# The first 128 tokens of expert 0 are gathered from three batches, and their two layers are issued inside the gating of the last batch

## Chip, cores, metric

The kernel runs on one core of a Trainium2 chip. The metric is the device time of one execution in microseconds; the kernel before has 881.16 us as the median of three runs (878.74 to 881.35). Its trace comes from one further execution under the profiler.

## What is computed

Three parts follow each other. Attention with a decay bias over 4 batches, 8 heads, 576 positions and 64 per head; its output is a matrix x of 2304 tokens by 512. Then a mixture of 8 experts in which every token goes to one expert, and its result is scaled by a gate:

```python
logits = x @ w_gate
e_idx = np.argmax(logits, axis=1)
...
for e in range(E):
    mask = e_idx == e
    h = np.maximum(x[mask] @ w1[e], 0.0)
    ye = h @ w2[e]
    out[mask] = gate_w[mask, None] * eom[mask, e, None] * ye
```

Here w1[e] is 512 x 1024 and w2[e] is 1024 x 512. Last, a feed-forward part over all tokens: h = x @ w_in (512 x 2048), g = relu(h) squared, out = g @ w_out. The weights w_in and w_out arrive as 64-bit floats.

## The kernel before

All matrix products that need precision run in three passes of reduced-precision fp32: each operand is split into a high part (a ScalarE copy) and a low part (a VectorE or GpSimd difference), and high x high, low x high and high x low are added in PSUM. That holds for weights (w_hi, w_lo; part_hi, part_lo), for x (x_hi, x_lo) and for h (emit_hv).

The order of the work is written out by hand. Every step is put on a list with `at(key, fn, ...)`, the list is sorted by key, and each engine executes its instructions in that order. One key unit is one attention unit (7 units per pair of heads, 16 pairs), later one block of 128 hidden columns (8 per expert). Engines wait for each other through semaphores; an instruction that waits holds up all that stand behind it in the queue of its engine.

Attention ends with the pair 15, whose units keep a different order (lorder, lpv). For each of batches 0 to 2 the gating runs beside later attention units: logits, argmax (s_mx to s_oh), the rank of a token within its expert (s_pr, s_tm, s_rk), a one-hot of the ranks (s_r1), and a matmul that turns it into a table of tokens by expert and rank (s_tb, s_tbl). carry holds the counts so far. For the last batch nothing is left to run beside. Its table is made in three parts of 128 ranks (chunks c = 0, 1, 2, five s_r1 compares and ten narrow matmuls each), each followed by a gather of that chunk of expert 0's rows of x. The rows come by an indirect DMA from GpSimd's queue out of x_d in DRAM, which attention has filled. The matmuls `warm` (keys tg + 0.0055 and + 0.0145) and `warm_h` multiply constants and their results are not read.

Then x_pe turns the gathered rows on TensorE, x_hi and x_lo split them, and perm_steps sorts the experts by load on VectorE: the order goes to slot_v, from where SyncE loads registers (load_regs) that address the weights and the output of experts 1 to 7. Expert 0 is always expert 0, so its weights are loaded and split during attention (part_load, part_hi, part_lo). Expert g takes CAPS[g] columns of tokens (352 for expert 0, 256 for the last); emit_h does a block of 128 hidden columns in 12 matmuls, with the weights stationary and the tokens moving; emit_y does the second layer likewise, 12 matmuls per block, and writes y transposed to yT_d. The weights of expert g+1 are loaded (w_load, three buffers stg and one stx), split and put into spare halves while expert g runs. Beside that, the 64-bit weights are turned into fp32 and stored (cv_load to cv_store), 16 pieces, every cvp units from cv0 on. A token above an expert's capacity is treated in a loop at the end of the kernel, which runs zero times for these data (p_max counts).

Of the kernel before, what the change touches and what calls it, by code (L numbers as in the profile page):

```python
# [71 lines left out]
    cvb=0.4,  # L72
    cvm=0.7,
    cvp=3.55,
    cv0=1.2,
# [12 lines left out]
def attention_moe_ffn_kernel(  # L88
# [72 lines left out]
    gap = const.tile([P, 1], F32, name="gap")  # L161
    slot_v = const.tile([1, 3, E], I32, name="slot_v")
# [117 lines left out]

    def gather(g, cs=None):
# [3 lines left out]
        for c, n in enumerate(rows_of(g)):  # L285
            if cs is not None and c not in cs:
                continue
            idx = tbl_i[0:n, c * E:c * E + 1] if g == 0 else tbl_p[0:n, c, g:g + 1]
# [13 lines left out]

    with tc.manual_schedule():
        with ExitStack() as actx:
# [7 lines left out]
            ps_s = actx.enter_context(tc.tile_pool(name="ps_s", bufs=K_["S"], space=PSUM))  # L312
            ps_t = actx.enter_context(tc.tile_pool(name="ps_t", bufs=6 - K_["S"] - K_["O"], space=PSUM))
            ps_o = actx.enter_context(tc.tile_pool(name="ps_o", bufs=K_["O"], space=PSUM)) if K_["O"] else ps_t
# [411 lines left out]
            def emit_gate(b, tg, gk):  # L726
# [36 lines left out]
                def s_pr():  # L763
                    pr = ps_o.tile([P, 512], F32, tag=o_tag, name=o_tag)
# [4 lines left out]
                    for t in range(NB - 1):  # L769
                        nc.tensor.matmul(  # L770
                            prv[:, t + 1:NB], lhsT=onesb, rhs=oh[:, t:t + 1].to_broadcast([P, NB - 1 - t, E]),
                            start=False, stop=(t == NB - 2))

# [12 lines left out]
                def s_r1(t, c0=0, c1=CH):  # L786
                    if t == 0 and c0 == 0:
# [4 lines left out]
                def s_tb(c0=0, c1=CH):  # L792
                    tb = T["tb", c0] = bank("o")
# [279 lines left out]
            for i, job in enumerate((k, i, h) for k, i in half_jobs(0, "a") + half_jobs(0, "b") for h in range(2)):  # L1073
# [3 lines left out]
                at(tw + 0.5, part_lo, *job)  # L1077
            emit_tasks()

        stg_p = ctx.enter_context(tc.tile_pool(name="stg", bufs=3))  # L1080
# [6 lines left out]
        ps_z = ctx.enter_context(tc.tile_pool(name="ps_z", bufs=1, space=PSUM))  # L1087
        ring = [4, 4, 0]

        def bank_z(i):  # L1090
            return ps_z.tile([P, 512], F32, tag=f"z{i}", name=f"z{i}")

        def bank_x():
            ring[2] += 1
            return bank_z(ring[0] + ring[2] % ring[1])

# [11 lines left out]
        xp_t = {}  # L1108

        def x_pe(g, c, k0=0, k1=KD):  # L1110
            if c == 0:
                xt_t[g] = xt_p.tile([P, 2, KD, TT], F32R, tag="xt", name="xt")
            r = rows_of(g)[c]
            ps = bank_x()
            for kk in range(k0, k1):
                nc.tensor.transpose(  # L1116
                    ps[:, (kk - k0) * r:(kk - k0 + 1) * r], xr_t[g][0:r, c, kk * P:(kk + 1) * P], ident[0:r, 0:r])
            xp_t[g, c, k0] = ps[:, 0:(k1 - k0) * r].rearrange("p (k n) -> p k n", k=k1 - k0)

# [558 lines left out]
```

## Time and profile before

| what | us |
|---|---|
| median of three runs | 881.16 |
| lowest and highest | 878.74, 881.35 |
| the profiled execution | 881.42 |
| its span, first to last instruction | 879.3 |
| TensorE busy in the span | 849.8 (97%) |
| VectorE busy | 517.9 (59%) |
| ScalarE busy | 447.8 (51%) |
| GpSimd busy | 256.2 (29%) |

All times in the rows count from the start of the span. PE is TensorE's matmuls, PEld its weight loads, DVE is VectorE, ACT ScalarE, POOL GpSimd, SP SyncE; a name with q is the engine's instruction queue. L with a number is a line of the kernel before. A busy engine of an average says little here, since the three parts of the kernel have different limits; what counts is which engine the others wait for in each stretch. The matmuls are pipelined, so the time of one is longer than the distance from one start to the next.

### The profile page before, as it was taken

How to read it: one execution, taken by the hardware profiler on the slowest of the kernel's cores; microseconds unless marked ns; L12 is line 12 of the kernel's file. 1: busy time of each engine (PE TensorE's matmuls, PEld its weight loads, DVE VectorE, ACT ScalarE, POOL GpSimd, SP SyncE). 2: the span in 40 equal slices, each digit the busy share in tenths (PEclk: the TensorE clock that was granted, in tenths of full speed). 3: DMA queues.
4: the chain of work that ended last, by engine and by line, in shares of the span. 5: the costliest groups of instructions: out<-in, count | busy, mean ns of one | idle time of the engine just before them, and what ended most of it. 6: DMA issues, size and time to landing. Idle time of an engine off the chain costs nothing.

```text
span 879.3 us, 15063 instructions
## 1 busy us (share of the span) xinstructions
PE 849.8 (97%) x5381; PEld 752.7 (86%) x5381; DVE 517.9 (59%) x1176; ACT 447.8 (51%) x995; POOL 256.2 (29%) x302
## 2 busy tenths in 40 slices
PE   8999999999899999999999999999999999999993
PEld 6877777776689999999999888999999999999993
DVE  8667877878666687777866565655323333322221
ACT  6787878887245556565655544444323222322221
POOL 4321344542125665566302233232001011001001
PEclk8999999999999999999999999999999999999997
DMA  6676677652178898988984332322102100000001
GB/s 157 140 161 139 151 184 177 163 135 76 48 252 269 247 254 238 276 264 271 287 235 123 101 114 72 108 77 92 46 28 72 37 37 37 1 1 37 0 1 39
DMA packets 112499, 113.12 MB, mean 129 GB/s; under 512 B 66017, under 2 KB 83425, under 8 KB 112418
## 3 DMA queue, kind: packets, MB, share of 16 engines
q1 hardware_dynamic: 106162, 97.23, 40.4%
q0 software_dynamic: 3664, 9.62, 3.3%
q10 hardware_dynamic: 2592, 5.24, 1.7%
q8 instruction: 44, 0.72, 0.4%
q14 instruction: 37, 0.30, 0.1%
HBM read 80.50 MB, written 23.32 MB: 118 GB/s over the span
## 4 chain that ended last, share of the span: by engine, by line
PE 44%; issue 30%; DVE 7%; ACT 7%; POOL 6%; DMA 5%; SPq 1%; POOLq 0%; DVEq 0%; ACTq 0%
PE z L1209 13%; PE z L1247 11%; PE s L483 5%; PE t L580 5%; PE t L543 4%; ACT p L527 2%; PE z L1256 2%; POOL out_dram L1316 2%; POOL cvm L1178 2%; POOL cvm L1177 2%; DMA w_in_d<-cvm 1%; DMA stg<-in_moe_w_dram 1%; ACT sta L423 1%; PE t L396 1%; PE z L1116 1%
## 5 line engine op out<-in xcount | busy, mean ns | idle before, releaser
L1209 PE MATMUL z<-xt,w 128*128 128x384 f32 (+6 forms) x1920 | 335.4, 323 | 3.5 <-DVE r L1227 2.3
L1209 PEld LDWEIGHTS z<-xt,w 128*128 128x128 f32 x1920 | 313.0, 188 | 12.9 <-DVE r L1227 3.2
L1256 PE MATMUL z<-w,h 128*128 128x512 f32 x864 | 215.5, 394 | 0.0
L1256 PEld LDWEIGHTS z<-w,h 128*128 128x128 f32 x864 | 161.4, 188 | 29.4
L1227 DVE SCALAR_TENSOR_TENSOR r<-z,r 128x384 f32<-128x384 f32 x96 | 53.3, 555 | 132.8 <-ACT r L1226 131.4
L1247 PE MATMUL z<-h,w 128*128 128x304 f32 (+5 forms) x768 | 115.0, 299 | 0.0
L1226 ACT ACTIVATE r<-z 128x384 f32<-128x384 f32 x96 | 46.9, 488 | 132.8 <-PE z L1209 130.0
L1247 PEld LDWEIGHTS z<-h,w 128*128 128x128 f32 x768 | 108.0, 188 | 0.0
L1177 POOL TENSOR_TENSOR cvm<-cvm,cva 128x512 f32<-128x512 f32 x32 | 43.7, 1364 | 204.5 <-DVE cva L1173 128.9
L1229 ACT CAST h<-r 128x384 fp32r<-128x384 f32 x96 | 49.3, 513 | 83.1 <-DVE r L1227 82.5
L1230 DVE TENSOR_TENSOR h<-r,h 128x384 fp32r<-128x384 f32 x96 | 58.2, 607 | 55.6 <-ACT h L1229 53.3
L1316 POOL DMA_INDIRECT out_dram<-ysb,tok_m x18 | 17.4, 968 | 239.5 <-ACT ysb L1303 177.2
L527 ACT ACTIVATE p<-p,nm 128x128 f32<-128x128 f32 (+3 forms) x144 | 84.2, 589 | 5.1 <-DVE nm L510 5.1
L510 DVE CUSTOM_DVE_ANT_0 p<-s,mask 128x128 f32<-128x128 f32 (+3 forms) x128 | 59.7, 485 | 28.9 <-PE s L483 27.9
L543 PE MATMUL t<-ident,p 128*128 128x128 f32 x400 | 69.3, 283 | 3.1 <-DVE sta L427 1.1
L245 DVE TENSOR_TENSOR w<-stg,w 128x1024 fp32r<-128x1024 f32 x49 | 69.5, 1419 | 0.5 <-ACT w L241 0.4
L543 PEld LDWEIGHTS t<-ident,p 128*128 128x128 f32 x400 | 44.7, 141 | 19.5 <-ACT p L527 6.7
L1178 POOL TENSOR_TENSOR cvm<-cvs,cvm 128x512 f32<-128x512 f32 x32 | 55.7, 1741 | 2.5
L241 ACT CAST w<-stg 128x1024 fp32r<-128x1024 f32 x49 | 51.3, 1046 | 8.9 <-DMA stg<-in_moe_w_dram 6.8
L1221 DVE SCALAR_TENSOR_TENSOR h<-z,h 128x304 fp32r<-128x304 f32 (+5 forms) x64 | 29.6, 462 | 44.1 <-ACT h L1220 40.9
L444 POOL CAST stb<-sta 64x1152 fp32r<-64x1152 f32 x28 | 31.4, 1149 | 79.5 <-PE s L483 47.1
L483 PE MATMUL s<-sta 128*64 128x288 f32 (+4 forms) x204 | 50.3, 344 | 2.7 <-ACT sta L423 1.1
(219 smaller groups left out, 1023.6 us busy)
## 6 DMA issues: line engine op xcount, KB each, us to landing
stg<-in_moe_w_dram SPq DMA_DIRECT2D x42, 512.0 KB
cv<-in_moe_w_out_dram SPq DMA_DIRECT2D x16, 512.0 KB
stx<-in_moe_w_dram SPq DMA_DIRECT2D x14, 512.0 KB
cv<-in_moe_w_in_dram SPq DMA_DIRECT2D x14, 512.0 KB
xr<-yT_d SPq DMA_DIRECT2D x8, 768.0 KB
qk<-in_q_dram SPq DMA_DIRECT2D x32, 128.0 KB
qk<-in_k_dram SPq DMA_DIRECT2D x32, 128.0 KB
v<-in_v_dram SPq DMA_DIRECT2D x32, 128.0 KB
```

The lines of the kernel that those rows point to most:

```text
L245: nc.vector.tensor_tensor(out=lo, in0=raw.pop(job), in1=hi.bitcast(F32), op=ALU.subtract)
L483: nc.tensor.matmul(ps[0:mw, d0:d0 + nn], lhsT=ql[r, m0:m0 + mw], rhs=kl[r, c0:c0 + nn], start=(i == 0 and (tail or n == 0)), stop=(done an ...
L510: nc.vector.tensor_tensor_reduce(out=dst, in0=src, in1=msk, scale=-1.0, scalar=3.0e38, op0=ALU.add, op1=ALU.min, accum_out=nm[:, c:c + 1])
L527: nc.scalar.activation(out=pt[:, cs], in_=pt[:, cs], func=AF.Exp, scale=-1.0, bias=nm[:, c:c + 1], accum_out=rs[:, r:r + 1])
L543: nc.tensor.transpose(tp[:, i * P:(i + 1) * P], pt[:, j0:j0 + P], ident)
L1177: nc.gpsimd.tensor_tensor(out=m, in0=m, in1=a.bitcast(F32), op=ALU.mult)
L1178: nc.gpsimd.tensor_tensor(out=m, in0=sq, in1=m, op=ALU.add)
L1209: nc.tensor.matmul(ps[:, 0:n], lhsT=wa[:, zw, kk, fl * P:(fl + 1) * P], rhs=xt[:, zx, kk, 0:n], start=(i == 0), stop=(i == 3 * KD - 1))
L1227: nc.vector.scalar_tensor_tensor(out=gg, in0=ps[:, 0:n], scalar=0.0, in1=gg, op0=ALU.max, op1=ALU.mult)
L1230: nc.vector.tensor_tensor(out=ht[:, 1, 0:n], in0=gg, in1=ht[:, 0, 0:n].bitcast(F32), op=ALU.subtract)
L1247: nc.tensor.matmul(y_acc[g][d][:, 0:n], lhsT=wb[:, zw, fl, d * P:(d + 1) * P], rhs=ht[:, zh, 0:n], start=(f == 0 and i == 0), stop=(f == n ...
L1256: nc.tensor.matmul(acc, lhsT=ht[:, zh, c * P:(c + 1) * P], rhs=wb[:, zw, fl, :], start=(first and i == 0), stop=(last and i == 2))
```

## The change

The index of expert 0's first 128 ranks (idx0) is copied from the table when batches 0 to 2 have been counted, and their rows are gathered then, from the part of x_d that those batches fill. The rows are turned and split (early_xt, early_xs) inside the last pair of attention, into buffers that attention no longer needs. Their first layer (early_h, two halves of 512 hidden columns, 12 matmuls each) and second layer (early_y, 24 matmuls) run with the tokens stationary and 512 weight columns moving. They are issued between the gating steps of the last batch in place of `warm` and `warm_h`, which are gone there. The table's chunks are made in the order 1, 2, 0; only chunks 1 and 2 are gathered there. In between stand the Relu (early_hr), the turning of h (early_ht) and its split (early_hs). The result is copied (early_copy), turned and stored on ScalarE's queue (early_store). Expert 0's own passes then have cols_of(0) = 224 columns. PSUM is regrouped for that before the gating of the last batch. seen0 keeps how many of expert 0's tokens were counted before the last batch; p_max gets one more test, whether that count was below 128. Further: conversions start at key 4.0 and come every 3.45; the first four weight loads of expert 1 have key -0.7; expert 1's x is turned 1.2 units later; perm_steps begin at -1.1 and the gather of expert 1 at -0.6.

```diff
     cvb=0.4,
+    ext=4.4,
     cvm=0.7,
-    cvp=3.55,
-    cv0=1.2,
+    cvp=3.45,
+    cv0=4.0,
...
+                idx = tbl_i[0:n, c * E:c * E + 1] if c else idx0
...
-                out=t[0:n, c, :], out_offset=None, in_=x_d[:, :],
+                out=t[0:n, c, :], out_offset=None, in_=x_d[:, :] if g or c else x_d[0:1 + (B - 1) * S, :],
...
-                steps = [s_lg, s_mx, s_eq, s_cand, s_ix, s_oh, s_pr, s_oid, s_tm, s_rk]
+                steps = [s_lg, s_mx, s_eq, s_cand, s_ix, s_oh]
                 if last:
+                    steps.append(partial(early_h, 0, 0, 9))
+                steps += [s_pr, s_oid, s_tm, s_rk]
+                if last:
+                    steps += [s_n3, partial(early_h, 0, 9, 3 * KD), partial(early_hr, 0), partial(early_h, 1, 0, 3)]
+                    after = {
+                        1: [partial(early_ht, 0), partial(early_h, 1, 3, 6)],
+                        2: [partial(early_h, 1, 6, 3 * KD), partial(early_hr, 1)],
+                        0: [partial(early_y, 0, 2)]}
                     ahead = 2
-                    for c in range(CH):
-                        steps += [partial(s_r1, t, c, c + 1) for t in range(ahead if c else 0, NB)]
+                    co = [1, 2, 0]
+                    for i, c in enumerate(co):
+                        steps += [partial(s_r1, t, c, c + 1) for t in range(ahead if i else 0, NB)]
                         steps.append(partial(s_tb, c, c + 1))
-                        if c + 1 < CH:
-                            steps += [partial(s_r1, t, c + 1, c + 2) for t in range(ahead)]
-                        steps += [partial(s_tbl, c, c + 1), partial(gather, 0, [c])]
+                        steps += after[c]
+                        if i + 1 < CH:
+                            steps += [partial(s_r1, t, co[i + 1], co[i + 1] + 1) for t in range(ahead)]
+                        steps.append(partial(s_tbl, c, c + 1))
+                        if c:
+                            steps.append(partial(gather, 0, [c]))
+                        if c == 2:
+                            steps.append(partial(early_hs, 0))
...
                     steps += rest[0:2]
+                    steps += [partial(x_pe, 0, 1), p_cnt, partial(early_ht, 1), partial(early_hs, 1)]
+                    steps += [partial(early_y, 2, FE // P), partial(x_pe, 0, 2)]
...
+                if b == B - 2:
+                    at(tg + gk[16] + 0.05, nc.vector.tensor_copy, idx0, tbl[:, 0:1])
+                    at(tg + gk[16] + 0.06, gather, 0, [0])
...
-                if last:
-                    at(tg + 0.0055, warm, K_["wm"][3])
-                    at(tg + 0.0145, warm, K_["wm"][4])
...
+            def early_h(half, i0, i1):
+                if i0 == 0:
+                    EA["h", half] = bank_z(3 + half)
+                wa = half_views((0, "a"))
+                seq = [(zw, zx, kk) for zw, zx in ((0, 0), (1, 0), (0, 1)) for kk in range(KD)]
+                for i in range(i0, i1):
+                    zw, zx, kk = seq[i]
+                    nc.tensor.matmul(
+                        EA["h", half], lhsT=x0[:, zx, kk], rhs=wa[:, zw, kk, 512 * half:512 * half + 512],
+                        start=(i == 0), stop=(i == 3 * KD - 1))
...
+            def early_hs(half):
+                ps = EA["t", half].rearrange("p (k n) -> p k n", k=4)
+                f = slice(4 * half, 4 * half + 4)
+                nc.scalar.copy(out=hT0[:, 0, f], in_=ps)
+                nc.vector.tensor_tensor(out=hT0[:, 1, f], in0=ps, in1=hT0[:, 0, f].bitcast(F32), op=ALU.subtract)
...
+            te = len(K_["order"]) * (NPAIR - 1)
+            at(te + K_["ext"], early_xt)
+            at(te + K_["ext"] + 0.1, early_xs)
...
         for i, fn in enumerate(first):
-            at((-0.9 if i < 1 else -0.75) + 0.001 * i, fn)
-        at(-0.74, load_regs, range(1, E), 0, reg_e, E - 1)
+            at(-1.1 + 0.001 * i, fn)
+        at(-1.05, load_regs, range(1, E), 0, reg_e, E - 1)
...
-        at(-1.1, warm_h, K_["wm"][5])
-        for c in range(CH):
-            x_trans(0, c, -1.0 + 0.1 * c)
-            at(-1.0 + 0.1 * c + 0.0015, warm_h, K_["wm"][6 + c])
-        at(0.3, gather, 1)
+        for c in (1, 2):
+            at(-1.0 + 0.1 * c, x_hi, 0, c)
+            at(-0.99 + 0.1 * c, x_lo, 0, c)
+        at(-0.85, early_copy)
+        at(-0.7, early_store)
+        at(-0.6, gather, 1)
...
-                    x_trans(g + 1, c, n0 + K_['xt0'] + K_['xt1'] * c, 0.3)
+                    x_trans(g + 1, c, n0 + K_['xt0'] + K_['xt1'] * c + (1.2 if g == 0 else 0.0), 0.3)
...
-                w_job(job, max(ta - K_["wld"], -0.7), ta + K_['wh'], ta + K_['wl'])
+                w_job(job, -0.7 if g == 0 and i < 4 else ta - K_["wld"], ta + K_['wh'], ta + K_['wl'])
```

## Rows read from the trace of the kernel before

**Rows 1.** Stretches: us; engines' busy us (instructions); TensorE clock, DMA share, GB/s.

```profile
230.73:234.14 3.41, 3.16 (x10) 1.46 (x9) 0.12 (x1) 0.31 (x1) 2.07 (x4) 0.50 0.68 185
248.00:256.00 8.00, 7.33 (x49) 6.82 (x47) 2.77 (x4) 2.57 (x5) 2.49 (x2) 1.00 0.97 340
...
257.30:268.97 11.67, 11.63 (x73) 11.63 (x74) 11.41 (x15) 7.60 (x13) 5.43 (x4) 1.00 0.59 192
268.97:297.00 28.03, 28.03 (x193) 27.77 (x193) 20.24 (x30) 15.13 (x26) 14.51 (x12) 1.00 0.87 266
```

**Rows 2.** The granted clock in 40 slices of the span, tenths.

```profile
PEclk8999999999999999999999999999999999999997
```

**Rows 3.** Timeline of TensorE: start, us, line, operation, count, [idle before].

```profile
223.91 2.32 PE L348 MATMUL t<-onesb 128*128 128x512 bf16 x10
...
227.77 0.63 PE L799 MATMUL t<-oid_all,r 128*128 128x8 bf16 x14
...
230.33 1.97 PE L1457 MATMUL z<-onesb 128*128 128x512 bf16 x5 [0.26 <-DVE tbl_i L808]
232.55 1.12 PE L1116 MATMUL z<-ident,xr 128*128 128x128 f32 x4 [0.25 <-DMA xr<-x_d,tbl_i]
...
237.81 6.15 PE L1209 MATMUL z<-xt,w 128*128 128x352 f32 x36
...
267.05 2.08 PE L1247 MATMUL z<-h,w 128*128 128x352 f32 x12
268.97 1.92 PE L1209 MATMUL z<-xt,w 128*128 128x320 f32 x12
```

**Rows 4.** Timelines of SyncE's queue, ScalarE and TensorE, expert 0.

```profile
244.50 5.02 SPq L232 DMA_DIRECT2D stg<-in_moe_w_dram  x3
...
254.84 1.05 ACT L241 CAST w<-stg 128x1024 fp32r<-128x1024 f32 x1 [5.43 <-DMA stg<-in_moe_w_dram]
...
257.34 2.19 PE L1209 MATMUL z<-xt,w 128*128 128x352 f32 x12 [1.18 <-DVE h L1221]
```

**Rows 5.** Timeline of TensorE, the last expert and the feed-forward part.

```profile
436.58 1.59 PE L1209 MATMUL z<-xt,w 128*128 128x256 f32 x12
438.00 1.67 PE L1247 MATMUL z<-h,w 128*128 128x272 f32 x12
...
499.62 2.01 PE L1256 MATMUL z<-w,h 128*128 128x512 f32 x8
501.47 2.25 PE L1209 MATMUL z<-xt,w 128*128 128x384 f32 x12
```

**Rows 6.** Timelines of TensorE and ScalarE in attention's tail.

```profile
217.22 0.76 PE L580 MATMUL t<-pt,v 128*64 128x320 f32 x4
218.01 0.58 ACT L562 COPY pt<-t 128x512 f32<-128x512 f32 x1 [0.87 <-PE t L580]
218.50 0.78 ACT L527 ACTIVATE p<-p,nm 128x576 f32<-128x576 f32 x1
218.68 0.63 PE L543 MATMUL t<-ident,p 128*128 128x128 f32 x4 [0.69 <-ACT pt L562]
```

**Rows 7.** Timelines of GpSimd and VectorE: carry, gather, order of the experts.

```profile
210.56 0.20 POOL L825 TENSOR_TENSOR carry<-carry,cs 128x8 f32<-128x8 f32 x1
...
228.92 1.22 POOL L289 DMA_INDIRECT xr<-x_d,tbl_i  x1 [2.44 <-DVE r L789]
...
236.93 0.15 DVE L1351 COPY ysb<-z 128x8 f32<-128x8 f32 x1
...
239.24 0.16 DVE L1385 CAST slot_v<-ysb 1x8 int32<-1x8 f32 x1
```

**Rows 8.** Timelines of VectorE and ScalarE: compares, and the splitting of x.

```profile
226.90 1.23 DVE L789 TENSOR_SCALAR r<-iota_r,rk_all 128x128 bf16<-128x128 f16 x7
...
233.83 0.58 ACT L1122 CAST xt<-z 128x512 fp32r<-128x512 f32 x1 [7.86 <-PE z L1116]
...
258.34 0.68 DVE L1127 TENSOR_TENSOR xt<-z,xt 128x512 fp32r<-128x512 f32 x1
```

More of the change, by code (lines that the diff above doesn't have):

```diff
@@ L301, in load_xf, with bank_z, bank_x, x_pe @@
             out=xf, in_=yT_d.rearrange("(k p) n -> p k n", p=P)[:, :, ds(c0, TT) if t else slice(0, TT)])
+    ring = [5, 3, 0]
+    zp = []
+    def bank_z(i):
+        return zp[0].tile([P, 512], F32, tag=f"z{i}", name=f"z{i}")
+    def bank_x():
+        ring[2] += 1
+        return bank_z(ring[0] + ring[2] % ring[1])
+    xp_t = {}
+    def x_pe(g, c, k0=0, k1=KD):
+        r = rows_of(g)[c]
+        ps = bank_x()
+        for kk in range(k0, k1):
+            nc.tensor.transpose(
+                ps[:, (kk - k0) * r:(kk - k0 + 1) * r], xr_t[g][0:r, c, kk * P:(kk + 1) * P], ident[0:r, 0:r])
+        xp_t[g, c, k0] = ps[:, 0:(k1 - k0) * r].rearrange("p (k n) -> p k n", k=k1 - k0)
+    R = {}
+    def p_cnt():
+        cps = bank_x()
+        nc.tensor.matmul(cps[:, 0:E], lhsT=onesb, rhs=carryb, start=True, stop=True)
+        R["cps"] = cps[:, 0:E]
     with tc.manual_schedule():
@@ L772, in s_pr, with s_n3 @@
                             start=False, stop=(t == NB - 2))
+                def s_n3():
+                    nc.scalar.copy(out=seen0, in_=T["pr"][0:1, 0, 0:1])
                 def s_oid():
@@ L786, in s_r1 @@
                 def s_r1(t, c0=0, c1=CH):
-                    if t == 0 and c0 == 0:
+                    if "r1" not in T:
                         T["r1"] = r1_p.tile([P, NB, CH * P], BF16, tag="r1", name="r1")
@@ L792, in s_tb @@
                 def s_tb(c0=0, c1=CH):
-                    tb = T["tb", c0] = bank("o")
+                    tb = T["tb", c0] = bank_x() if last else bank("o")
                     nz = 2 if last else 1
@@ new lines, in attention_moe_ffn_kernel, with early_xt, early_xs @@
+            hT0 = early_view(st_a[(NPAIR - 3) % 3], [2, FE // P, P])
+            def early_xt():
+                ps = EA["x"] = bank("s")
+                for kk in range(KD):
+                    nc.tensor.transpose(ps[:, kk * P:(kk + 1) * P], xr_t[0][:, 0, kk * P:(kk + 1) * P], ident)
+            def early_xs():
+                ps = EA["x"].rearrange("p (k n) -> p k n", k=KD)
+                nc.scalar.copy(out=x0[:, 0], in_=ps)
+                nc.vector.tensor_tensor(out=x0[:, 1], in0=ps, in1=x0[:, 0].bitcast(F32), op=ALU.subtract)
@@ new lines, in early_hr, with early_ht @@
+            def early_hr(half):
+                EA["r", half] = qk_p.tile([P, 2 * QM + 2 * D], F32, tag="qk", name="qk")[:, 0:512]
+                nc.scalar.activation(out=EA["r", half], in_=EA["h", half], func=AF.Relu)
+            def early_ht(half):
+                ps = EA["t", half] = bank_z(half)
+                for i in range(4):
+                    nc.tensor.transpose(ps[:, i * P:(i + 1) * P], EA["r", half][:, i * P:(i + 1) * P], ident)
+            def early_hs(half):
[3 more added lines that the diff above has]
+                nc.vector.tensor_tensor(out=hT0[:, 1, f], in0=ps, in1=hT0[:, 0, f].bitcast(F32), op=ALU.subtract)
@@ new lines, in early_y @@
+            def early_y(f0, f1):
+                if f0 == 0:
+                    xp_t["y"] = bank_z(2)
+                wb = half_views((0, "b"))
+                for f in range(f0, f1):
+                    for i, (zh, zw) in enumerate(((0, 0), (0, 1), (1, 0))):
+                        nc.tensor.matmul(
+                            xp_t["y"], lhsT=hT0[:, zh, f], rhs=wb[:, zw, f, :],
+                            start=(f == 0 and i == 0), stop=(f == FE // P - 1 and i == 2))
+            te = len(K_["order"]) * (NPAIR - 1)
@@ L1106, in attention_moe_ffn_kernel, with x_hi @@
         h_t = {}
-        xp_t = {}
-        def x_pe(g, c, k0=0, k1=KD):
-            if c == 0:
+        def x_hi(g, c, k0=0, k1=KD):
+            if c == first_of(g):
                 xt_t[g] = xt_p.tile([P, 2, KD, TT], F32R, tag="xt", name="xt")
             r = rows_of(g)[c]
[L1114 to L1118, printed above, removed]
-        def x_hi(g, c, k0=0, k1=KD):
-            r = rows_of(g)[c]
-            nc.scalar.copy(out=xt_t[g][:, 0, k0:k1, c * P:c * P + r], in_=xp_t[g, c, k0])
+            n0 = (c - first_of(g)) * P
+            nc.scalar.copy(out=xt_t[g][:, 0, k0:k1, n0:n0 + r], in_=xp_t[g, c, k0])
         def x_lo(g, c, k0=0, k1=KD):
@@ L1201, in emit_h @@
         def emit_h(g, e, f, fl):
-            n = sum(rows_of(g))
+            n = cols_of(g)
             xt = xt_t[g]
@@ L1215, in emit_hv @@
         def emit_hv(g, f):
-            n = sum(rows_of(g))
+            n = cols_of(g)
             ps = hp_t.pop((g, f))
```

77 lines of the change are left out of this document (46 added, 31 removed).

## The prediction

> **What bounds the kernel now.** I read the stretches first. From 268.97 us on, where the second expert begins, TensorE is busy 28.03 of 28.03 us at clock 1.00, and VectorE 20.24 [rows 1]; the slices of the granted clock show one low patch in the middle [rows 2]. So whatever moves the start of the second expert moves the end by as much, unless another engine becomes its bound. The timeline of TensorE around the gating comes next. Its last work for attention is issued at about 223.9; from there to 237.81, 13.9 us, it runs constant bf16 matmuls that compute nothing, the small matmuls of rank and table and twelve transposes; from 237.81 come expert 0's 352-wide passes, and the second expert starts at 268.97 [rows 3]. That is the room the change wants to fill. In it the clock is at its lower level, 0.50, from 230.73 to 234.14 [rows 1].
>
> The stage of expert 0 is not all work. Up to 268.97 it issues 168 of its 192 wide matmuls at 0.160 us (26.9) and twelve transposes of x (about 1.2): 28.1 of 31.16 us, so 3.1 us are stalls. One shows: the pass at 257.34 waited for VectorE's part of an earlier h, that for ScalarE's, and ScalarE had sat 5.43 us in front of a weight that was still on its way, though the queue had issued it from 244.50 [rows 4], while the DMA engines were busy 0.97 at 340 GB/s [rows 1].
>
> **What a matmul costs.** From start to start: 352 columns 0.160 us (267.05 to 268.97, twelve), 256 columns 0.118 (436.58 to 438.00, twelve), 512 columns 0.231 (499.62 to 501.47, eight) [rows 3, 5]. A 128-wide transpose is about 0.12 (four in 0.63, the last one 0.27 long) [rows 6]. No 224-wide pass is in the trace. Above, it cannot cost more than the 0.118 of the wider one; below, the slope from 352 to 256 (0.00044 per column) gives 0.104. A floor seems near, since 128 columns cost no less than 0.11; I take 0.112. The Trainium skill, "TensorE: Matmul & The Clock Gate", section "Back-to-back issue gap", gives the gap at full clock as N/2.4 + 2.5 ns, which is 0.096 for 224 columns, an estimate from that page; by it the saving below would be 12.3 instead of 9.2 us. The rows lie some 10 ns above it at 352 and 256, so the rows decide.
>
> **Term 1, columns taken out of the wide passes.** Expert 0 has 96 first-layer and 96 second-layer passes; each falls from 352 to 224 columns: 192 x (0.160 - 0.112) = 9.2 us less (8.1 by 0.118, 10.8 by 0.104). The 48 new 512-wide matmuls cost 48 x 0.231 = 11.1 us, but stand mostly in the 13.9 us of room, where 29 constant matmuls go.
>
> **Term 2, the first wide pass comes later.** In times of the kernel before:
>
> (a) Attention's tail. The gather of the first 128 rows goes to POOL behind the carry of batch 2, about 211; 1.22 us of POOL and a landing some 3.6 us after its start (228.92 to the transposes at 232.5) put the rows there by 215, in time [rows 7]. The two POOL steps queued behind it, and a VectorE sum that waits for them, slip 1.2 us; VectorE has about as much idle time right after, so I count nothing (cover gone: 0.4). The four transposes of these rows come behind the P.V pass issued to 217.86, in a TensorE gap of 0.69 us, hidden. But their ScalarE copy (0.58) is queued ahead of the copy at 218.01, which TensorE waits for at 218.68 [rows 6]. It can begin at about 218.45, so the copy behind it ends at 219.6 instead of 218.6, and the exponential and last transposes behind it: +1.0 us (bounds 0 and 1.3). The VectorE difference falls in an idle moment.
>
> (b) The gating. h half 0, nine passes (2.1 us), takes the place of ten constant matmuls (2.3), then three, the rank, and three of half 1 in place of seven: no loss. The second table (ranks 128 to 255) is built first. Then the queues bite. ScalarE must do the Relu of half 1 before it copies the turned half 0. Half 1's last passes are issued behind the third table, 229.5 to 230.9; Relu to 231.75, copy to 232.2, VectorE's difference (0.68) to 232.95, and only behind that stand three of the five compares of the first table [rows 7, 8]. So that table, which second-layer passes stand behind on TensorE, is ready at 233.5: TensorE idles about 2.5 us, where it formerly waited for gathers. Then in its queue: six second-layer passes (1.4) to 234.9, four transposes, four more of h half 1 to 235.8, eighteen passes (4.2) to 240.0, the transposes of the third rows to 240.3. ScalarE now copies y (0.58) to 240.85 before the hi part of those rows, to 241.3; four transposes of y go beside it. First wide pass: 241.4, against 237.81: +3.6 (2.5 if ScalarE's queue runs as much ahead as it can, 4.5 if each wait adds 0.1). The other gathers are not later and are covered.
>
> (c) The clock. It fell at 230.73 after a sparse stretch (the tables' narrow matmuls from 227.8 on) and stayed at half for 3.41 us [rows 1, 2]. The idle 2.5 us is a like case, and the constant matmuls are gone. A half stretch like that costs at most 1.7 us, none costs nothing; nothing in the trace chooses, I take the middle, 0.8.
>
> Sum: +5.4, first wide pass at 243.2.
>
> **Term 3, stalls in expert 0's stage.** The order of experts is computed on VectorE in the 3.5 us from 236.93, and slot_v at 239.24 feeds the register loads that precede the weight loads [rows 7]. Now it stands behind the difference of h half 1 (to 237.35, plus 1.0 and 0.8): the first load is issued near 246.5 instead of 244.5. Four instead of two go out before the second series of register loads, so the third comes at about 247, not 249. The conversions of the FFN weights start 2.8 steps later and free ScalarE, VectorE and 0.5 MB of DMA here. In the queues until four loads have landed: 2.1 MB of weights, 0.66 of gathers, 0.26 of the early store, 0.5 of FFN weights, 3.5 MB at 340 GB/s: 10.3 us, about 255 to 257 for the last. The second, which held ScalarE until 254.84, I put at 254.5. ScalarE's hi part (1.05), its queue, and VectorE's part then let h pass 5 start about 2.4 us later, at 256.9 (the interval was 254.84 to 257.34) [rows 4]. Unstalled it would start at 243.2 + 5 x 1.34 + 3 x 1.34 = 254.0. From there to the second expert are 72 passes, 8.1 us, but VectorE, busy 11.41 of 11.67 us in that stretch [rows 1], drops only to some 9: the second expert starts near 265.7. That is 243.2 + 20.0 of work + 2.5 of stalls; 0.5 to 4.5 are possible. Against 3.1: -0.6.
>
> **Sum.** -9.2 + 5.4 - 0.6 = -4.4 us. The profiled execution took 881.42 us (span 879.3 and 2.1 around it), so 877.0; the median of the three runs is 0.26 lower: 876.8. The two added checks on VectorE (0.15 us each), the smaller stores and h parts lie beside TensorE and count nothing.
>
> **Rivals.**
> A, the lower clock lasts through the second layer: 24 passes at 0.231 become 0.427 (five constant 512-wide ones took 1.97 us mostly at half [rows 3]), and with the transposes 5.9 us more than unslowed. First wide pass 248.3; the weights are then there, stalls 0.5: -9.2 + 10.5 - 2.6 = -1.3, 880. For: the constant matmuls go. Against: between 234.14 and 237.8 the clock stayed up through gaps as well.
> B, on the slower side: the four loads share the DMA engines and land together. The Trainium skill, "DMA: Bandwidth & Descriptors", section "Issuing engines are not separate DMA queues", says that transfers run on the same 16 DMA engines and interleave whichever engine started them. By that rule an earlier issue buys no bandwidth; the share of 0.97 at 340 GB/s agrees [rows 1]. If the second lands with the fourth at 258, h pass 5 starts at 260.4, and VectorE, with all its differences and conversions behind that point, needs its former 11.4 us: second expert at 271.8, 2.8 later than before, less 1.1 us for the 24 narrower passes that follow: +1.7, 883. It becomes slower when the second load lands after 256.3. For: in the trace it took ten us from its issue. Against: the second FFN load is out of its way.
> C, no clock loss, loads that land in turn (second by 252), stalls 0.5: -9.2 + 4.6 - 2.6 = -7.2; with the low price of a pass -8.8: 872.5 to 874.
>
> **Chances.** Forecast (875 to 879.5) 0.60, A 0.13, B 0.14, C 0.13. Over 0.3% (2.6 us, about what runs of this kernel can tell from no change) faster: C, most of the forecast, a little of A: 0.70. Slower by that: the worse half of B with (a) and (b) at their bounds: 0.10. Within: 0.20. Range 872 to 882.5: it leaves out about 0.08 below (C with every bound good) and 0.10 above.
>
> **What would show it.** A 224-wide pass every 0.112 us; ScalarE's copy at 218.0 a microsecond late; TensorE idle for 2 to 3 us behind h half 1 until the first table; first wide pass at 242 to 244; a patch of clock 0.5 near it; h pass 5 behind a weight near 254 to 255; second expert near 265.7. I am wrong if wide passes start before 240 or the second expert after 269, or if TensorE waits for weights later than that.

## The result, and the profile of the changed kernel

The changed kernel takes **888.79 us** (median of 14 runs, 883.05 to 894.87) against 880.47 (14 runs, 878.74 to 883.15) of the kernel before on the same chip: ratio **1.0094, 95% interval 1.0077 to 1.0112**. It is slower. Predicted were 876.8 us, in a range of 872 to 882.5.

The profiled execution took 891.59 us, 2.8 above the median; the stages below add up to its span. "Predicted" are the prediction's own terms: 188.1 is the time before less 1.1 for 24 narrower passes, and the feed-forward part is taken as unchanged.

| stage, us of the span | before | predicted | after |
|---|---|---|---|
| start to expert 0's first wide pass | 237.81 | 243.2 | 247.48 |
| expert 0's stage | 31.16 | 22.5 | 26.88 |
| second expert to feed-forward part | 189.25 | 188.1 | 196.72 |
| feed-forward part to the end | 421.1 | 421.1 | 418.8 |
| span | 879.3 | 874.9 | 889.9 |

The clock first. On the page of the changed kernel, two more of the 40 slices are at 8 than in [rows 2], the eleventh and twelfth (222 to 267 us):

```profile
span 889.9 us, 15145 instructions
PEclk8999999999889999999999999999999999999997
```

The same as stretches: gating, expert 0's stage, the other experts (columns as in rows 1), and behind them the two stretches of the gating that lie wholly at the lower level, 0.50.

```profile
224.70:247.50 22.80, 18.53 (x110) 14.20 (x108) 10.69 (x54) 6.02 (x18) 2.25 (x3) 0.85 0.12 34
247.50:274.36 26.86, 23.68 (x183) 23.13 (x181) 16.71 (x47) 12.34 (x23) 9.36 (x11) 0.87 0.68 218
274.36:471.08 196.72, 190.08 (x1427) 188.59 (x1426) 150.47 (x194) 112.86 (x188) 100.74 (x86) 0.99 0.88 257
...
228.07:231.48 3.41, 3.41 (x15) 2.41 (x14) 0.84 (x5) 0.15 (x1) 0.00 (x0) 0.50 0.11 26
238.31:241.72 3.41, 3.41 (x12) 2.65 (x12) 0.61 (x4) 0.00 (x0) 0.00 (x0) 0.50 0.00 0
```

In the kernel before, the third of these stretches had no idle TensorE at all:

```profile
268.97:458.22 189.25, 189.25 (x1426) 188.15 (x1426) 138.88 (x187) 110.86 (x186) 95.23 (x84) 1.00 0.88 259
```

The timeline of TensorE answers to [rows 3, 4]. Read the numbers in brackets: they are where it stood still.

```profile
224.71 0.31 PE L660 MATMUL s<-wp,oT 128*128 128x32 f32 x2
226.99 3.31 PE L967 MATMUL z<-w,sta 128*128 128x512 f32 x9 [1.97 <-ACT xs L701]
230.10 0.26 PE L806 MATMUL z<-carryb,onesb 128*128 128x40 bf16 x1
...
235.52 0.26 PE L842 MATMUL z<-oid_all,r 128*128 128x8 bf16 x4
237.73 0.53 PE L842 MATMUL z<-oid_all,r 128*128 128x8 bf16 x6 [1.96 <-DVE r L832]
238.12 2.74 PE L992 MATMUL z<-w,sta 128*128 128x512 f32 x6
...
247.48 1.69 PE L1314 MATMUL z<-xt,w 128*128 128x224 f32 x13
...
253.19 1.15 PE L1352 MATMUL z<-h,w 128*128 128x224 f32 x8 [1.45 <-ACT h L1325]
256.07 1.20 PE L1352 MATMUL z<-h,w 128*128 128x224 f32 x4 [1.74 <-DVE h L1326]
...
273.02 1.50 PE L1352 MATMUL z<-h,w 128*128 128x224 f32 x12
274.36 1.93 PE L1314 MATMUL z<-xt,w 128*128 128x320 f32 x12
...
292.10 0.45 PE L331 MATMUL z<-ident,xr 48*128 48x48 f32 x4
294.80 2.31 PE L1314 MATMUL z<-xt,w 128*128 128x320 f32 x12 [2.25 <-DVE h L1326]
```

Each standstill has its cause on another engine. For 226.99 the row names it: h half 0 waits for the last of ScalarE's ten `xs` copies, which read attention's banks, not h's. For 237.73 VectorE shows that the difference of h's turned half 0 (L984) stands ahead of the last three compares (L832), and that slot_v is 6.6 us later than in [rows 7]; the first weight loads go out behind it, at 251.29:

```profile
236.82 0.69 DVE L984 TENSOR_TENSOR sta<-z,sta 128x512 fp32r<-128x512 f32 x1 [2.42 <-ACT sta L983]
237.43 0.57 DVE L832 TENSOR_SCALAR r<-iota_r,rk_all 128x128 bf16<-128x128 f16 x3
...
245.85 0.16 DVE L1483 CAST slot_v<-ysb 1x8 int32<-1x8 f32 x1
...
251.29 1.49 SPq L235 DMA_DIRECT2D stg<-in_moe_w_dram  x3
```

For 253 to 256 GpSimd comes first: the three gathers of the second expert (L301) stand ahead of its step of the loss (L873), for which ScalarE waits (L883) with h queued behind it (its row names no releaser; the same wait in experiment a1, below, names GpSimd's `dl`):

```profile
248.48 0.96 POOL L301 DMA_INDIRECT xr<-x_d,tbl_p  x1 [12.87 <-ACT h L1562]
249.74 0.95 POOL L301 DMA_INDIRECT xr<-x_d,tbl_p  x1 [0.30 <-issue]
251.00 0.92 POOL L301 DMA_INDIRECT xr<-x_d,tbl_p  x1 [0.30 <-issue]
251.94 0.27 POOL L873 TENSOR_TENSOR dl<-lgl,mx 128x40 f32<-128x40 f32 x1
```

```profile
252.24 0.24 ACT L883 ACTIVATE pe<-dl 128x40 f32<-128x40 f32 x1 [3.89 <-issue]
252.68 0.21 ACT L885 ACTIVATE ez<-zs 128x5 f32<-128x5 f32 x1 [0.21 <-issue]
252.79 0.34 ACT L1325 ACTIVATE h<-z 128x224 fp32r<-128x224 f32 x1
...
256.24 1.04 ACT L244 CAST w<-stg 128x1024 fp32r<-128x1024 f32 x1 [2.63 <-DMA stg<-in_moe_w_dram]
...
292.75 0.66 ACT L1270 ACTIVATE cvm<-cv 128x512 f32<-128x512 uint16 x1 [5.33 <-DMA w_in_d<-cvm]
293.31 0.57 ACT L1226 CAST xt<-z 128x512 fp32r<-128x512 f32 x1
293.78 0.44 ACT L1325 ACTIVATE h<-z 128x320 fp32r<-128x320 f32 x1
```

The last three of these rows belong to 294.80. ScalarE's part of a weight conversion writes `cvm`, which has one buffer, and waits until the piece before is stored; h waits behind it. How long such a store of 256 KB takes differs: ScalarE's queue issued this one at 281.75 and ScalarE went on at 292.75, 11.0 us later, but 3.6 us after the one issued at 358.75. What makes one store three times as long as another the rows don't show; the DMA engines were busy 0.88 over the other experts' stages. ScalarE's waits over the other experts' stages (engine, line and what it waited for: us in all, times, longest), first of the changed kernel, then of the kernel before:

```profile
ACT cvm L1270 <- DMA w_out_d<-cvm: 10.4, 6, 5.4
ACT cvm L1270 <- DMA w_in_d<-cvm: 9.0, 5, 5.3
```

```profile
ACT cvm L1165 <- DMA w_out_d<-cvm: 6.2, 5, 2.2
```

### The profile page after: what moved, and what is told of

It is laid out like the page before. It is cut to its first block, busy times and chain, and to the rows that moved or that the text cites. A ratio compares the mean times of both kernels' runs of the same rounds, so it can differ in the third digit from the quotient of the medians.

```text
span 889.9 us, 15145 instructions
## 1 busy us (share of the span) xinstructions
PE 852.1 (96%) x5412; PEld 755.2 (85%) x5412; DVE 524.5 (59%) x1180; ACT 450.4 (51%) x1002; POOL 260.0 (29%) x302
## 4 chain that ended last, share of the span: by engine, by line
PE 39%; issue 30%; DVE 9%; ACT 8%; POOL 7%; DMA 5%; SPq 0%; POOLq 0%; ACTq 0%; DVEq 0%
PE z L1314 10%; PE z L1352 10%; PE s L523 5%; PE t L620 5%; PE t L583 4%; POOL cvm L1283 2%; DMA w_out_d<-cvm 2%; POOL cvm L1282 2%; POOL out_dram L1421 2%; ACT p L567 2%; DMA w_in_d<-cvm 2%; DVE cvs L1276 1%; DVE r L1332 1%; PE t L436 1%; ACT sta L463 1%
## 5 line engine op out<-in xcount | busy, mean ns | idle before, releaser
L1314 PE MATMUL z<-xt,w 128*128 128x384 f32 (+6 forms) x1920 | 331.4, 321 | 7.9 <-DVE h L1326 6.6
L1314 PEld LDWEIGHTS z<-xt,w 128*128 128x128 f32 x1920 | 308.9, 189 | 18.0 <-DVE h L1326 7.1
L248 DVE TENSOR_TENSOR w<-stg,w 128x1024 fp32r<-128x1024 f32 x49 | 75.1, 1533 | 1.0 <-ACT w L244 0.9
```

The lines of the kernel that those rows point to most:

```text
L248: nc.vector.tensor_tensor(out=lo, in0=raw.pop(job), in1=hi.bitcast(F32), op=ALU.subtract)
L1314: nc.tensor.matmul(ps[:, 0:n], lhsT=wa[:, zw, kk, fl * P:(fl + 1) * P], rhs=xt[:, zx, kk, 0:n], start=(i == 0), stop=(i == 3 * KD - 1))
```

## The experiments

All of them were timed in five rounds beside the kernel before, in three sets; the kernel before stood at 880.75, 880.17 and 880.24 us in them.

| | median us (range, runs) | ratio to before, 95% interval |
|---|---|---|
| changed kernel | 888.79 (883.05 to 894.87, 14) | 1.0094, 1.0077 to 1.0112 |
| a1 conversions back | 888.21 (886.50 to 891.17, 6) | 1.0091, 1.0074 to 1.0109 |
| a2 before, conversions moved | 883.90 (880.40 to 887.30, 12) | 1.0038, 1.0021 to 1.0055 |
| a3 gather 1 later | 886.13 (883.61 to 889.39, 6) | 1.0067, 1.0045 to 1.0088 |
| a4 banks by tile | 885.09 (881.08 to 891.43, 12) | 1.0057, 1.0032 to 1.0082 |
| b1 a3 and a4 | 885.66 (876.33 to 889.43, 7) | 1.0067, 1.0044 to 1.0090 |
| c conversions' wait moved | 882.25 (877.35 to 883.55, 12) | 1.0014, 1.0001 to 1.0027 |
| d all mends | 872.63 (871.54 to 874.94, 5) | 0.9918, 0.9905 to 0.9931 |
| e before, conversions' wait moved | 877.62 (877.02 to 880.57, 8) | 0.9979, 0.9967 to 0.9990 |
| f TensorE kept busy | 889.15 (882.46 to 891.66, 7) | 1.0075, 1.0047 to 1.0103 |
| g difference behind compares | 884.32 (880.14 to 886.49, 9) | 1.0046, 1.0029 to 1.0064 |
| h a3, a4 and g | 879.68 (875.64 to 883.96, 12) | 0.9988, 0.9967 to 1.0008 |
| i d, transposes later | 872.31 (871.51 to 872.80, 5) | 0.9911, 0.9899 to 0.9924 |

A second reading of the runs is used from here on. Each run has a span and a mean granted clock; span x (1 - clock) is the time that the lower clock took if TensorE was at work all through, span x clock the rest. Means: before 9.4 and 869.5 (the 23 runs beside the a set), changed kernel 14.8 and 872.2. So of the 8 us, some 5.5 are the clock's and 2.8 are not. Runs of one kernel differ by several us, so a difference of 2 or 3 us between medians of six to twelve runs is near what can be told.

**a1 and a2, the places of the conversions.** The change spaces them by 3.45 instead of 3.55 passes and starts them at 4.0 instead of 1.2. Undone in the changed kernel (a1), done alone in the kernel before (a2):

```diff
-    cvp=3.45,
+    cvp=3.55,
-    cv0=4.0,
+    cv0=1.2,
```

> The changed kernel with the conversions of the 64-bit weights at their former places (cv0=1.2, cvp=3.55), all else as changed. Theory: the TensorE gaps of 2.5, 2.9 and 2.0 us near 292, 380 and 406 us come from the new places of the conversions (ScalarE waits for the store of the piece before, and h waits behind it); they go, and the time falls from 888.8 to 883-885.5. Rival: the gaps come from the weight loads that move with expert 0's stage; they stay, 888-890.

> The kernel before with only cv0=4.0 and cvp=3.45, nothing else changed. Theory: the new places alone make ScalarE wait for stores between 270 and 460 us and cost 3 to 6 us: 883.5-886.5 against 880.5, with TensorE gaps of over 2 us. Rival: they do no harm where the rest is unchanged: 880-881.5.

a2: 3.2 to 3.4 us slower, as expected. TensorE waits 1.07 and 2.47 us ahead of 371.90 and 397.63, behind VectorE's part of h, where the kernel before waits for nothing. a1: the gaps behind the second expert went as expected, but the total stayed at the rival's 888, because expert 0's stage took 32.7 us (244.22 to 276.91) instead of 26.9. Its ScalarE waits, over that stage, say why:

```profile
ACT cvs L1266 <- DMA cv<-in_moe_w_in_dram: 8.6, 1, 8.6
ACT xt L1226 <- PE z L331: 3.9, 3, 2.0
ACT pe L883 <- POOL dl L873: 3.9, 1, 3.9
```

The early conversion waits 8.6 us for its load, issued beside the four weight loads, and h waits behind it; 13.7 us of the stage (252.3 to 266.0) ran at the lower clock, against 6.8 in the changed kernel. By the second reading the rest fell by 2.6 us and the clock's part rose by 2.2. The late places cost the other experts, the early ones expert 0: putting the constants back was no cure. The first wide pass came 3.3 us earlier here (244.22), though nothing ahead of it had changed: both standstills of the gating were there (2.0 us each), and the clock stayed at 1.00 behind them.

**a3, GpSimd's order.**

```diff
-        at(-0.6, gather, 1)
+        at(-0.4, gather, 1)
```

> The changed kernel with the gather of expert 1 issued behind the late gating steps (key -0.4 instead of -0.6), so that GpSimd's subtraction no longer stands behind three gathers. Theory: the 4 us in which ScalarE and VectorE stand idle after 248 us go, the second layer of expert 0 no longer waits 1.5 and 1.7 us, the second expert starts 3 to 5 us earlier: 883.5-886. Rival: the landing of expert 1's weights sets that stage anyway: 888-889.5.

2.7 us fall by the medians; the intervals of the two ratios overlap. ScalarE's 3.89 us ahead of L883 become 0.51, expert 0's stage takes 24.64 us instead of 26.88, and the second expert starts at 270.50. (Another 1.6 us of that come ahead of the stage, where nothing was changed: the clock held behind the wait for the compares in this execution.) But the gather is then late for the transposes of the second expert's tokens:

```profile
252.70 1.50 PE L1352 MATMUL z<-h,w 128*128 128x224 f32 x12
256.66 0.66 PE L331 MATMUL z<-ident,xr 128*128 128x128 f32 x4 [2.46 <-DMA xr<-x_d,tbl_p]
```

**a4, the wait for banks.** The new pool of banks is allocated over attention's pools; here each tile waits for the last user of its own bank instead of for all users of those pools.

```diff
-            zp.append(ctx.enter_context(tc.tile_pool(name="ps_z", bufs=1, space=PSUM)))
+            zp.append(ctx.enter_context(tc.tile_pool(name="ps_z", bufs=1, space=PSUM, reuse_waits="tile")))
```

> The changed kernel with the new PSUM pool waiting bank by bank for earlier users instead of for all users of attention's pools. Theory: h half 0 no longer waits 2 us for ScalarE's last scaling of x, starts near 225 us instead of 227.0, the rank follows the argmax at once (228 instead of 230.1), and the first wide pass comes 2 to 4 us earlier (243.5-245.5): 884.5-887. Rival: the wait is one for the bank itself or the clock falls as before in the gaps behind; start of the wide passes unchanged within 1 us: 888-889.5.

3.7 us fall by the medians; here too the intervals overlap. h half 0 follows attention's last matmul without a gap, and the rank comes at 227.10, where the prediction's terms give about 227; the wait for the compares stays as it was.

```profile
224.80 0.31 PE L660 MATMUL s<-wp,oT 128*128 128x32 f32 x2
224.95 2.31 PE L967 MATMUL z<-w,sta 128*128 128x512 f32 x9
227.10 0.19 PE L806 MATMUL z<-carryb,onesb 128*128 128x40 bf16 x1
...
234.15 0.53 PE L842 MATMUL z<-oid_all,r 128*128 128x8 bf16 x6 [1.96 <-DVE r L832]
```

**b1, a3 and a4 together.**

> The changed kernel with both mends at once: the bank pool waits tile by tile (alone 885.1, 3.7 below the changed kernel's 888.8) and the gather of expert 1 is issued after GpSimd's step of the loss (alone 886.1, 2.7 below). Theory (two separate places of loss, one ahead of the first wide pass and one behind the eighth): they add, 888.8 - 3.7 - 2.7 = 882.4, range 881 to 884; first wide pass near 243.5, second expert near 267.5. Rival (both losses end in one thing, the lower clock and the late weight loads of expert 0's stage, so the second mend finds nothing left): 884.5 to 886, second expert near 270.5 as with either mend alone.

By the median the two do not add, and the rival's number was met. In the profiled execution, the fastest of the seven, they do: the second expert starts at 265.70, where the theory had 267.5 and the rival 270.5. But the runs lie 13 us apart, and the clock accounts for it: granted 0.993 in the run of 876.33, 0.980 in that of 889.43, while span x clock lies within 868.1 to 872.5 in all seven. Against the changed kernel the rest fell from 872.2 to 869.4 (a3 alone 870.5, a4 alone 870.5), the clock's part only from 14.8 to 13.5.

**c and e, the conversions' wait.** ScalarE's and GpSimd's intermediate results go to the low words of the loaded piece, which has two buffers; only GpSimd's last add writes `cvm`, so the wait for the store falls to GpSimd. c is the changed kernel with this edit, e the kernel before with it.

```diff
-            nc.scalar.activation(out=cv[n][3], in_=cv[n][4], func=AF.Copy, scale=2.0 ** -36)
+            nc.scalar.activation(out=cv[n][0].bitcast(F32)[:, :, 0], in_=cv[n][4], func=AF.Copy, scale=2.0 ** -36)
...
-            nc.gpsimd.tensor_tensor(out=m, in0=m, in1=a.bitcast(F32), op=ALU.mult)
-            nc.gpsimd.tensor_tensor(out=m, in0=sq, in1=m, op=ALU.add)
+            u = t.bitcast(F32)[:, :, 0]
+            nc.gpsimd.tensor_tensor(out=u, in0=u, in1=a.bitcast(F32), op=ALU.mult)
+            nc.gpsimd.tensor_tensor(out=m, in0=sq, in1=u, op=ALU.add)
```

> The changed kernel with one difference: ScalarE's scaled copy of each weight conversion (line 1270) and GpSimd's multiply write into the low words of the loaded piece, which has two buffers, and only GpSimd's last add writes cvm, so that GpSimd and not ScalarE waits for the store of the piece before. Nothing moves. Theory (the stores' wait on ScalarE holds h, and so the second-layer matmuls, three times in experts 2 to 8): the gaps at 292, 380 and 406 (2.5, 2.9 and 2.0 us) shrink to under 1.2 us and the stretch from the second expert to the start of the dense tiles falls from 196.7 by 4 to 7; total 882.5 to 885. Rival (the stores are late because the DMA engines are full there, and weight loads or gathers then hold the same passes): gaps of 2 us and more remain at other places behind DMA waits of w_hi or the gathers; total 887 to 889.

> The kernel before with the conversions' edit alone (ScalarE no longer waits for the store of the piece before). Theory: ScalarE's waits for these stores were 7.5 us in all in this kernel, with no TensorE gap over 1.2 us behind them between 269 and 500, so 0 to 2 us fall: 878.5 to 880.5. Rival (the edit is worth as much here as in the changed kernel, so that it tells nothing of the change): 4 us or more, under 877.

c: 6.5 us fall, a little more than expected, and the stretch of the other experts is without an idle moment again (196.72 to 188.26):

```profile
274.57:462.83 188.26, 188.26 (x1426) 187.15 (x1425) 152.85 (x194) 112.62 (x188) 102.21 (x86) 1.00 0.90 267
```

188.26 is also what the prediction had (188.1): the 24 narrower passes are there. e: 2.6 us fall by the medians, 1.8 by the ratio, between the theory (0 to 2) and the rival (4): the edit is worth something for its own sake, and about 4 us more in the changed kernel.

**f and g, the idle stretches of the gating.** f fills both with constant matmuls and moves nothing; g takes the second away.

```diff
+            at(NU * (NPAIR - 1) + K_["lpv"][0][-1] + K_["xe"] + 0.01 - 2e-6, warm, 10)
...
+                        if c == 0:
+                            steps.append(partial(warm_z, 9))
                         steps.append(partial(s_tb, c, c + 1))
```

```diff
-                        1: [partial(early_ht, 0), partial(early_h, 1, 3, 6)],
+                        1: [partial(early_ht, 0), partial(early_h, 1, 3, 6), partial(early_hs, 0, 0)],
...
+                        if c == 0:
+                            steps.append(partial(early_hs, 0, 1))
                         steps.append(partial(s_tb, c, c + 1))
...
-                        if c == 2:
-                            steps.append(partial(early_hs, 0))
```

(In g, early_hs(0, 0) is ScalarE's copy alone and early_hs(0, 1) VectorE's difference alone.)

> The changed kernel with TensorE kept busy in its two idle stretches of the last gating, and nothing moved: ten constant 512-column matmuls behind the last tile of the attention, ahead of the wait for the banks, and nine ahead of table 0. They feed nothing. Read by two numbers for each run, both from its span and mean granted clock: span x (1 - clock) is the time taken by the lower clock (changed kernel 14.8 us mean of 14 runs, kernel before 9.4 of 23), span x clock is the rest (872.2 against 869.5). Theory (5 of the change's 8 us are the clock, and it falls because TensorE stands idle 2.2 and 2.1 us there): the clock's share falls to 9 to 11, the rest stays at 872 to 873; total 882.5 to 885. Rival (the clock falls for the later gaps at 248 to 256 and in experts 2 to 8, or by chance): its share stays at 14 to 15; total 887.5 to 889.5.

> The changed kernel with early_hs(0) in two parts: ScalarE's copy right behind its transposes, VectorE's difference behind the three compares of table 0 and no longer ahead of them. Theory (the 2.1 us of TensorE ahead of table 0 come from that difference): the gap at 235.6 shrinks to under 0.8 us, the first wide pass moves from 247.5 to 245 to 246, total 886 to 887.5; with the clock's share lower by one stretch of 3.4 us at half speed (1.7 us), 884.5 to 886. Rival (gather 1 ahead of the loss step and the weight loads set the passes of expert 0 in any case): the first wide pass moves, the second expert does not (274 to 274.5); total 888 to 889.

f: in the profiled run the clock stays up through the whole gating, and the first wide pass comes 2.3 us earlier, though the useful matmuls start no sooner.

```profile
224.70:245.21 20.51, 20.05 (x133) 14.31 (x133) 10.88 (x54) 6.02 (x18) 2.25 (x3) 1.00 0.13 38
245.21:271.87 26.66, 23.48 (x183) 22.93 (x182) 16.73 (x47) 12.34 (x23) 9.36 (x11) 0.87 0.68 219
271.87:470.89 199.02, 191.99 (x1426) 190.26 (x1425) 147.21 (x194) 112.85 (x188) 101.45 (x86) 0.98 0.88 253
```

The total did not follow: 889.15, the rival's number. Expert 0's stage and the others kept their gaps and their low clock, and the others took 2.3 us more than in the changed kernel's profile. Over the runs the clock's part is 12.0, between theory (9 to 11) and rival (14 to 15), the rest 873.8. One execution does not show that the constants held the clock up, since a1 held it through the same two standstills without them. All the profiles of the changed kernel and its variants together say more. Behind the wait for banks the clock fell in four of the five executions that have it (not in a1), behind the wait for the compares in three of six (not in a1, a3 and b1); where the wait was gone, or filled as in f, it fell in none of six and none of five. So the clock falls there with the standstills, though not each time. What that is worth to the total, f does not settle. g: 4.5 us fall, just past the better end of the theory (884.5). Table 0 is issued in one piece and the first wide pass comes at 242.92, the second expert at 269.38, so the rival is out:

```profile
234.85 0.41 PE L842 MATMUL z<-oid_all,r 128*128 128x8 bf16 x10
235.11 1.64 PE L994 MATMUL z<-w,sta 128*128 128x512 f32 x6
```

**h, d and i, the mends together.** h has a3, a4 and g; d has c as well; i is d with the second expert's transposes 0.8 of a pass later.

> The kernel with both mends (banks tile by tile, gather 1 later: 885.7 median, 876.3 to 889.4 from run to run) and early_hs(0) in two parts. Theory (its spread is the clock, which falls in some runs for the idle stretch ahead of table 0): the clock's share falls from 13.5 to 8 to 10 us, the rest from 869.4 by 1 to 2; total 877 to 879.5, runs within 4 us of each other. Rival (the clock falls for the gaps behind the conversions in experts 2 to 8, which stay): share 12 to 14, total 882 to 885, spread as before.

> All mends at once: banks wait tile by tile, gather 1 later, conversions as in the run before, and of early_hs(0) the ScalarE copy issued right after its transposes while VectorE's difference stands behind the three compares of table 0. Theory: 882.4 (both mends) minus 4 to 6 for the conversions, minus 1.5 to 2.5 for the 2.1 us gap of TensorE at the first table: 875 to 877.5, below the kernel before (880.5). Rival (what is gained ahead of expert 0 is lost in its stage to the weight loads, whose times hang on registers and queues and not on these places): 879 to 882, no faster than the kernel before.

> The kernel with all four mends (872.6) and the transposes of the second expert's tokens issued 0.8 of a pass later, so that TensorE does not meet gather 1 at 248.2 (2.5 us idle, 2.2 of them behind that transfer). Theory: 1 to 2.2 us fall, 870.5 to 872. Rival (the transposes come too late for the second expert or meet other work, and h waits in their place): 872.5 to 875.

h: level with the kernel before. The clock's part is 10.8, a little above the theory, and the runs still lie 8 us apart; waits of 2.29 and 2.78 us remain ahead of 369.03 and 395.08, behind VectorE's part of h. So b1's spread was not the compares' gap alone. d: without those gaps too it is 8.5 (the rest 862.5), the runs lie within 3.4 us, and the kernel is **0.8% faster than the kernel before**, 2.4 us below the expected range. Its stretches:

```profile
224.40:240.12 15.72, 14.93 (x109) 11.59 (x107) 10.53 (x53) 6.04 (x18) 2.75 (x5) 1.00 0.18 49
240.12:263.88 23.76, 20.83 (x184) 20.27 (x182) 16.32 (x47) 12.15 (x24) 8.72 (x9) 1.00 0.75 243
263.88:452.00 188.12, 188.12 (x1426) 187.01 (x1425) 153.94 (x194) 112.81 (x189) 102.30 (x86) 1.00 0.89 269
```

i is not to be told from d. The 2.2 us behind the gather are gone, and h waits in their place, as the rival said. What holds h is a weight: ScalarE sits 6.77 us in front of a load that is still on its way, until 249.65, and h stands behind it in its queue.

```profile
PE z L1355 <- ACT h L1328: 1.7, 1, 1.7
PE z L1317 <- DVE h L1329: 1.3, 1, 1.3
```

## Why the prediction was wrong

The sum was 15.0 us short of the profiled span: 4.3 at the first wide pass, 4.4 in expert 0's stage, 8.6 in the other experts, and 2.3 the other way in the feed-forward part, where the kernel before had 3.4 us at the lower clock (534.5 to 537.9), a cost of 1.7, and the changed kernel had none.

**Right.** Term 1: a 224-wide pass costs 0.112 us (273.02 to 274.36, twelve), as taken. The Trainium skill, "TensorE: Matmul & The Clock Gate", section "Back-to-back issue gap", gives N/2.4 + 2.5 ns for an isolated matmul, an estimate of 0.096 here, and says itself that this counts too little at small N when weight loads stand between the matmuls. The measurement is 0.016 above, so the rows were the better guide. Term 2 (a), in part: attention's last matmuls are issued 0.95 us later (224.71 against 223.76), where 1.0 was forecast for ScalarE's copy; but 0.36 of that stands in the trace already at 210 us, ahead of the copy. Of (b), the three compares behind VectorE's difference: 1.96 us of idle TensorE against 2.5. Of the size: d is 5.0 us faster than e, the kernel before with the same edit of the conversions; forecast were 4.4. That is a near hit for the design and not for the kernel, since d also lacks the 1.96 us at the compares, which the forecast had in it.

**Step 1 that failed: Term 2 (b), "h half 0 ... takes the place of ten constant matmuls ... no loss".** It waited 1.97 us for banks that it does not use. The constant matmuls ran in attention's own banks. The prediction's own rows may have had the sign: the first matmul of the new pool, at 230.33, waits for VectorE's `tbl_i`, which reads a bank of attention [rows 3]; whether that was the bank written, the rows don't say. The wait was 0.26 us and I passed over it; h half 0 is moved to a place where the wait for attention's readers is long. a4: 3.7 us.

**Step 2: Term 2 (c), the clock, 0.8 us.** Two stretches of 3.4 us at 1.2 GHz lie in the gating (228.07 to 231.48 and 238.31 to 241.72), each right behind a standstill of TensorE of 2 us, and two more stretches later, 6.8 us from 255.38 and 3.4 from 296.34, again behind standstills. I counted half of one, 0.8 of the 3.4 us that the two in the gating cost (each 1.7, half its length). I read a low patch in the middle of [rows 2]; there is none, only the first and the last slice are lower. The slices are 22 us long, and one stretch of 3.4 does not show in them. In the profiles the clock falls in the gating only where one of the two standstills is, but not each time (see f), so the 3.4 us hold for the profiled execution and not for every run. Steps 1 and 2 with the shorter wait at the compares make up the first wide pass: 2.0 later at h half 0 (226.99 against 224.95 in a4), 3.4 - 0.8 = 2.6 for the clock, 0.5 less at the compares: 4.1 of the 4.3.

**Step 3: Term 3, stalls of 2.5 us in expert 0's stage.** I looked for the holder in the weight loads, which I let start at 246.5; they started at 251.29, and yet the first standstills, at 253.19 and 256.07, are behind GpSimd's gathers and the steps of the loss that they hold back. The queues had been worked out for ScalarE and VectorE; on GpSimd the gather of the second expert, ahead of the loss, was not followed. By the rows this stage has 3.2 us of idle TensorE (1.45 and 1.74; counted from start to start 3.7) and 3.1 of the lower clock (6.8 us at half, in 0.7 of which TensorE stood still), against 2.5 in all: 4.3 of the 4.4. a3 makes the stage 2.2 us shorter; the rest turns into a wait for the gather's landing. The weight load that I had named was next in line: with the gathers out of the way, in i, it holds h for 1.75 us.

**Step 4: Term 3, "The conversions of the FFN weights start 2.8 steps later and free ScalarE".** The new start and spacing were read for expert 0 alone. Everywhere else they set when ScalarE's `cvm` step comes after the store of the piece before, and three times h stood behind it: 2.25 us at 294.80 and 6.6 in all three, and 1.7 for the clock at 296.34: 8.3 of the 8.6. The prediction gave the other experts no term but the 24 narrower passes. It had also said that it would be wrong "if TensorE waits for weights later than that"; it waited later, but behind a store. c: 6.5 us, of which e shows 2.6 in the kernel before as well; a2: the new places alone cost 3.2 there. And the sentence that a moved start of the second expert moves the end by as much held only as long as VectorE and ScalarE kept up: [rows 1] shows TensorE full there, but a full engine says nothing of how long the waits beside it may grow before they show.

**The rivals.** A named the clock, in one long stretch in the second layer; it fell in four shorter ones. B had the slower side for weights that land together; in the changed kernel no row shows TensorE held by them. Slower had a chance of 0.10, and the four steps were all errors to one side. In two of them a moved instruction was costed at nothing: h half 0 ahead of the wait for banks, and the second expert's gather ahead of the loss.

The four mends alone give 3.7, 4.5, 2.7 and 6.5 us (a4, g, a3, c), 17.4 in sum; together they give 16.2. That they add so nearly is partly luck: by the median a3 and a4 together did not, and part of c's gain is there without the change. What each is worth without the clock can't be read closer than the 2 to 3 us by which the clock differs from run to run.

## What to carry to other kernels

Follow a moved instruction on every in-order queue, GpSimd's too, and ask not only what it needs but what it now stands in front of. A periodic side job with one buffer has its slack set by its phase: when its start or spacing is changed, check the wait on that buffer over the whole kernel, not in the stage that the change is about. Where a new pool is laid over an old one, look whose reader its first tile waits for: if that reader used another bank, the wait belongs to the pool (a4 took it away), and it grows when the work behind it is moved forward.

## What the runs showed of the hardware that was not expected

The granted clock differs from run to run of one kernel, and more in the variants whose TensorE has standstills of about 2 us. Seven runs of b1 went from 876.33 us (mean clock 0.993) to 889.43 (0.980) with the rest of the time within 4.4 us, while 23 runs of the kernel before lie within 4.1 in all. A standstill does not always bring the clock down: in a1 both standstills of the gating were passed at full clock, and so were d's 2.2 us behind the gather, up to 250.66. The kernels with fewer standstills were not only faster but steadier: five runs of i lie within 1.3 us and five of d within 3.4, the fourteen of the changed kernel within 11.8. Why a standstill is passed at full clock in one execution and not in another, the runs don't show.
